# Row transform by pairs of column halves: a spectral layer and an MLP with all their gradients on one core

## The chip, the cores and the metric

The kernel runs on one NeuronCore of one Trainium2 chip. The core has five engines that run side by side, each with its own list of instructions: TensorE for matrix products (PE in the profile; its weight loads are listed as PEld), VectorE (DVE), ScalarE (ACT), GpSimd (POOL) and SyncE (SP). The last three also issue DMA transfers from their queues. The metric is the time of one execution on the device in microseconds; the kernel before takes 1196.34 us (median of 3 runs, 1196.11 to 1196.62).

## The reference

Two branches are computed from their inputs, mixed row by row by a sigmoid gate, and then everything is differentiated. S = 2048 rows, D = 1024 columns, F = 3584 hidden units; bf16 in and out.

```python
def _A_ref(x, w_r, w_i):
    X = rfft2(x.astype(float32), axes=(-2, -1))
    X = X * (w_r + 1j * w_i)                      # w: 2048 x 513
    return irfft2(X, s=(S, D), axes=(-2, -1)).astype(bfloat16)

def _B_ref(x, w1, b1, w2, b2):
    h = einsum("bsd,df->bsf", x, w1) + b1
    r = where(h > 0, h, 0)
    return einsum("bsf,fd->bsd", r * r, w2) + b2

x = A_x                                           # both branches read it; B_x is not used
g = sigmoid((x * gate_w).sum(-1, keepdims=True))
out = g * _A_ref(x, A_w_r, A_w_i) + (1 - g) * _B_ref(x, B_w1, B_b1, B_w2, B_b2)
_out, _vjp = jax.vjp(_f, A_x, A_w_r, A_w_i, B_w1, B_b1, B_w2, B_b2, gate_w)
return (_out, *_vjp(grad_out))
```

So nine arrays leave the kernel: the output and the gradients of x, of both filters, of the four MLP weights and biases, and of the gate.

## The kernel before

The two-dimensional Fourier transform is taken apart into small matrix products. Its stages run as a side task beside the MLP, which is the main task:

1. `first_stage` transforms x and the gated gradient along the columns and does the first part of the row transform; the result goes to a scratch array in HBM, `z_scr`.
2. `fft_mid` (line 333) does the rest of the row transform, multiplies by the filter, makes the gradient of the filter, and transforms back; its result goes to `y_scr`. **This is the stage that changes.**
3. `fft_out` reads `y_scr`, finishes the back transform and writes `ax_scr`, which the last stage (`Outputs`) adds to the MLP's result.

The MLP's main task is `mlp_in` (hidden layer and its gradient; products named ph, pZ and pd in the profile) until about 465 us, then `mlp_grads` (weight gradients; pX and pV), then `Outputs` (xX, xV, xZ). All three use a scheme of seven block products in place of eight, for which VectorE forms sums of operands (lines 873 and 1138) and joins of results. In `mlp_in` VectorE also makes each dhT (line 787, which frees the bank of a pd) and rT (line 900); ScalarE copies parts out of PSUM (cu, u: line 888) and squares (line 751).

The side task is a generator. `spread` advances it by a number of steps for every step of the main task: 1.5 side steps per main step while `fft_mid` runs beside `mlp_in` (`first_rate`), 1.2 times the main step's weight beside `mlp_grads` (`rate`). The tile framework then orders the recorded instructions for each engine and sets the semaphores. On each engine the instructions run in that order: one that waits holds up all behind it. A tile with a tag and `bufs=n` has n buffers that are used in turn; who writes a buffer again waits until its readers are done, DMA stores included.

`fft_mid` handles 16 pairs of row frequencies, m = 0 to 15, and each in two halves of the columns, h = 1 and then h = 0: 32 turns. A turn is:

- `inputs` (line 397): two DMAs on ScalarE's queue bring z for (m, h), two turns ahead.
- `mirrored` (line 419): on VectorE, sum and difference of the two parts of z into a tile pm (line 425; for m = 0, z itself).
- `transform` (line 430): four products px on TensorE, each of 128 partitions onto 64 (line 435), in a bank pair `ps2`; then ScalarE copies them out as x, once plain, once with the sign turned (lines 436 to 438).
- `by_groups` (line 407): GpSimd puts the filter's half in order (w), with its negative.
- `products` (line 441) and `joined` (line 449): VectorE multiplies x by w (two instructions, tt) and adds (y). The half h = 1 has one extra column, which is handed to h = 0 through eh.
- `back` (line 461): four products pv, each of 64 partitions onto 128 (line 466), in a bank pair `ps2`; ScalarE copies half of them (vc), VectorE makes sum and difference (pc, lines 472 and 473), GpSimd's queue stores them in `y_scr`.
- `grads_of_w` (line 478) and `grads_out` (line 489): VectorE multiplies and adds (g, gs), ScalarE scales into gw, and after h = 0 four stores on GpSimd's queue write the gradient of the filters.
- `filters` (line 388), once per m: five loads on GpSimd's queue, of the transform matrices (ab) and the filter rows (wn) for the next m.

The PSUM tag `ps2` has two buffers, and px and pv of all turns share them. `back` of a turn is issued in the next turn, so the order of TensorE's groups is px of turn u, then pv of turn u - 1, with products of the MLP between them nearly always.

Of the kernel before, what the change touches and what calls it, by code (L numbers as in the profile page):

```python
# [141 lines left out]
def kernel(  # L142
# [190 lines left out]
    def fft_mid(filler):  # L333
# [16 lines left out]
        def edges_through(ams):  # L350
            flat = lambda t_: t_[:].rearrange("p a b l -> p (a b l)")
            parted = fb.tile([P, 2, 2, HW], FDT, name="parted", tag="pm")
            parted = flat(parted)[:, 0 : 4 * P].rearrange("p (e k i) -> p e k i", e=4, i=NT)
            of_edge = edge[:].rearrange("p x t i -> p (x t) i").unsqueeze(2).to_broadcast([P, 4, 8, NT])
# [4 lines left out]
            for e in range(4):  # L359
                mm(pe[:, e, :], lhsT=parted[:, e].rearrange("p k i -> p (k i)"), rhs=row_of[:], start=True, stop=True, skip_group_check=True)  # L360
            ed = fb.tile([P, 2, 2, HW], FDT, name="ed", tag="y")
            ed = flat(ed)[:, 0 : NM * 8].rearrange("p (m n e) -> p m n e", n=2, e=4)
# [56 lines left out]
        def mirrored(m, z, summed=None):  # L419

            if m == 0:
                return z
            pm = fb.tile([P, 2, 2, HW], FDT, name="pm", tag="pm")
            for n, op in enumerate((ALU.add, ALU.subtract)):
                mixed = V(out=pm[:, n], in0=z[:, 0], in1=z[:, 1], op=op)
                behind(mixed, "DVE")
                after(mixed, summed, mybir.DependencyClass.NoSync)
            return pm

        def transform(m, h, pm, ex):  # L430
            x = fb.tile([P, 3, 2, WL], FDT, name="x", tag="x", bufs=2)
            px = fps.tile([P, 2, 2, HW], FP32, name="px", tag="ps2", bufs=2)
            for c in range(2):
                for n in range(2):
                    behind(mm(px[lanes[n], c], lhsT=mats[m][:, 0, n, lanes[c]], rhs=pm[:, n], start=True, stop=True), "PE")  # L435
            nc.scalar.copy(out=x[:, 1:3, :, 0:HW], in_=px[:])
            copied = nc.scalar.mul(out=x[:, 0, :, 0:HW], in_=px[:, 1], mul=-1.0)
            nc.scalar.copy(out=x[:, :, :, h * HW], in_=ex[:, m, :, :, h])
            return x, copied
# [9 lines left out]
        def joined(h, tt, eh):  # L449
            y = fb.tile([P, 2, 2, HW], FDT, name="y", tag="y")  # L450
            V(out=y[:], in0=tt[:, 0, :, :, 0:HW], in1=tt[:, 1, :, :, 0:HW], op=ALU.add)
# [8 lines left out]

        def back(m, h, y):
            pc = fb.tile([P, 2, 2, HW], FDT, name="pc", tag="pc", bufs=2)
            pv = fps.tile([P, 2, 2, HW], FP32, name="pv", tag="ps2", bufs=2)
            for c in range(2):
                for n in (1, 0):
                    mm(pv[:, n], lhsT=mats[m][lanes[n], 1, c, :], rhs=y[lanes[n], c], start=c == 0, stop=c == 1)
            if m == 0:
                done = nc.scalar.copy(out=pc[:], in_=pv[:])
            else:
                vc = fb.tile([P, 2, HW], FP32, name="vc", tag="vc")  # L470
                done = nc.scalar.copy(out=vc[:], in_=pv[:, 1])
                V(out=pc[:, 0], in0=pv[:, 0], in1=vc[:], op=ALU.add)  # L472
                V(out=pc[:, 1], in0=pv[:, 0], in1=vc[:], op=ALU.subtract)
# [28 lines left out]
        ams = [some_am(0), some_am(1)]  # L502
        turns = [(m, h) for m in range(NM) for h in (1, 0)]
        z = {0: inputs(*turns[0])}
        later["mid"] = True
# [4 lines left out]
        for _ in filler:  # L510
            yield
        pm, w = mirrored(0, z.pop(0)), by_groups(1, wn[0])
        held = eh = gw = summed = None
        z[1] = inputs(*turns[1])
        yield
        for u, (m, h) in enumerate(turns):
            if h:
                eh = fb.tile([P, 2, 2], FDT, name="eh", tag="eh")
            x, copied = transform(m, h, pm, ex)
            if u + 2 < len(turns):  # L520
                z[u + 2] = inputs(*turns[u + 2], copied)
            yield
            if u + 1 < len(turns):
                pm = mirrored(turns[u + 1][0], z.pop(u + 1), summed)
            if held:
                done = back(*turns[u - 1], held)
            tt = products(h, x, w)
            if u + 1 < len(turns):
                m2, h2 = turns[u + 1]
                w = by_groups(h2, wn[m2])  # L530
            yield
            held = joined(h, tt, eh)
            yield
            if u:
                grads_out(*turns[u - 1], gs, gw, done)
            gs, summed = grads_of_w(h, x)
            if h:
                gw = fb.tile([P, 2, LW], BF16, name="gw", tag="gw", bufs=2)
                if m + 1 < NM:
                    wn[m + 1] = filters(m + 1)  # L540
            yield
        done = back(*turns[-1], held)
        grads_out(*turns[-1], gs, gw, done)
        yield
# [1373 lines left out]
```

## Time and profile before

| | |
|---|---|
| time, median of 3 runs | 1196.34 us |
| the profiled execution's own time | 1203.86 us |
| its span, first to last instruction | 1202.1 us |
| granted clock of TensorE | 0.999 |
| PE busy | 1179.5 us |
| DVE busy | 893.5 us |
| ACT busy | 535.8 us |
| POOL busy | 375.9 us |
| px, first and last start | 232.3 and 582.6 us |
| pv, first and last start | 242.6 and 596.0 us |
| px products | 128, four to a turn |
| pv products | 128, four to a turn |

One execution is recorded by the profiler. Matrix products overlap: each is listed with its whole duration (379 ns for one with 512 columns), while the next starts 216 ns after it; so distances between starts tell more than the busy time. In the lists of groups, a name such as pd<-dbT,w2T says which tile is written from which; L783 is line 783. "Idle" is the time that an engine sat before an instruction, with what ended it.

### The profile page before, as it was taken

The page shows a single profiled execution, that of the slowest core. Times are in us where ns is not written, and L with a number is a line of the kernel's source. Part 1 is how long each engine was busy: PE and PEld are TensorE (multiplying, and loading weights), DVE is VectorE, ACT ScalarE, POOL GpSimd, SP SyncE. Part 2 cuts the span into 40 slices and gives each one's busy share as a digit, 9 for nine tenths or more (in the row PEclk, how much of TensorE's full clock was granted, in tenths as well). Part 3 has the DMA queues.
Part 4 walks back from the last instruction along what each step waited for, and adds up shares of the span by engine and source line. Part 5 has one row for each costly group of instructions (what it writes and reads, how often), then busy time and mean ns, then how long its engine had stood idle before and what let it go on. Part 6 is the DMA issues. An engine that isn't in the chain of part 4 may idle for free.

```text
span 1202.1 us, 19429 instructions
## 1 busy us (share of the span) xinstructions
PE 1179.5 (98%) x7181; PEld 636.1 (53%) x7275; DVE 893.5 (74%) x1598; ACT 535.8 (45%) x961; POOL 375.9 (31%) x618
## 2 busy tenths in 40 slices
PE   8989999999999999999999999999999999999998
PEld 5555555443333444444446899999544444444444
DVE  5878887689898887776637666666786677986757
ACT  5657888576767783444414556564201010000000
POOL 0224433665666663553322322321001100000000
PEclk9999999999999999999999999999999999999999
DMA  9998585686969888989897999994889999665530
GB/s 242 295 237 244 179 210 185 203 200 192 220 189 212 246 243 174 206 183 220 202 225 141 232 218 249 252 208 151 258 170 251 270 255 280 192 188 153 179 123 36
DMA packets 329464, 249.84 MB, mean 208 GB/s; under 512 B 187912, under 2 KB 287658, under 8 KB 328858
## 3 DMA queue, kind: packets, MB, share of 16 engines
q1 hardware_dynamic: 268352, 112.12, 44.8%
q0 software_dynamic: 35136, 111.72, 29.4%
q10 hardware_dynamic: 25882, 24.76, 7.3%
q8 instruction: 57, 0.93, 0.3%
q14 instruction: 37, 0.30, 0.1%
HBM read 114.82 MB, written 89.67 MB: 170 GB/s over the span
## 4 chain that ended last, share of the span: by engine, by line
PE 73%; DVE 12%; DMA 5%; ACT 4%; issue 4%; SPq 1%; POOL 0%; ACTq 0%; another core or an unknown queue 0%; DVEq 0%; POOLq 0%
PE pX L1206 15%; PE xX L1505 13%; PE pV L1206 11%; PE pd L783 8%; PE xV L1505 6%; PE ph L884 6%; PE xZ L1505 3%; DMA dhT_scr<-dhT 1%; PE pui L325 1%; DVE rT L900 1%; PE ph L776 1%; PE pki L591 1%; PE px L435 1%; DVE dhT L787 1%; DMA z<-z_scr 1%
## 5 line engine op out<-in xcount | busy, mean ns | idle before, releaser
L783 PE MATMUL pd<-dbT,w2T 128*128 128x512 bf16 x859 | 205.4, 379 | 4.4 <-DMA w2T<-in_B_w_dram 2.0
L783 PEld LDWEIGHTS <-w2T 128*128 128x128 bf16 x896 | 86.3, 98 | 106.4 <-issue 3.9
L1505 PEld LDWEIGHTS <-dS 128*128 128x128 f16 x686 | 66.3, 98 | 79.1 <-issue 3.4
L787 DVE SCALAR_TENSOR_TENSOR dhT<-pd,rT 128x512 bf16<-128x512 f32 x112 | 76.6, 684 | 32.7 <-PE pd L783 26.0
L1556 POOL DMA_DIRECT2D out_dram<-ot x32 | 17.3, 542 | 249.4 <-DVE ot L1612 128.0
L1622 ACT ACTIVATE w2br<-w2br,dsc 128x512 f32<-128x512 bf16 x8 | 5.8, 722 | 175.0 <-DVE ot L1612 117.4
L1222 ACT COPY u<-pX 128x512 f32<-128x512 f32 x56 | 32.8, 585 | 98.7 <-PE pX L1206 92.6
L1505 PE MATMUL xX<-oT,dS 128*128 128x512 f16 x336 | 76.5, 379 | 0.2 <-DVE eR L1534 0.2
L1505 PEld LDWEIGHTS <-odd 128*128 128x128 bf16 (+1 forms) x462 | 44.8, 98 | 51.5 <-issue 0.9
L1505 PEld LDWEIGHTS <-even 128*128 128x128 bf16 (+1 forms) x448 | 43.6, 98 | 52.6 <-issue 0.7
L1206 PEld LDWEIGHTS <-T 128*128 128x128 f16 x672 | 64.7, 98 | 7.9 <-issue 0.7
L901 ACT ACTIVATE rT<-rT 128x512 bf16<-128x512 bf16 x69 | 43.3, 628 | 40.7 <-DVE rT L900 40.7
L751 ACT ACTIVATE h2T<-rT 128x1024 bf16<-128x1024 bf16 x56 | 59.7, 1065 | 0.5 <-issue 0.2
L1226 DVE TENSOR_TENSOR whi<-pV,u 128x512 bf16<-128x512 f32 x28 | 19.3, 690 | 51.6 <-ACT u L1222 48.1
L475 POOL DMA_DIRECT2D y_scr<-pc x64 | 46.9, 734 | 34.4 <-DVE pc L472 31.9
L446 DVE TENSOR_TENSOR tt<-x,w 128x1028 f16<-128x1028 f16 (+1 forms) x64 | 41.9, 691 | 17.0 <-issue 12.5
L1206 PEld LDWEIGHTS <-S 128*128 128x128 f16 x336 | 32.3, 98 | 41.0 <-DVE S L1138 1.3
L1206 PEld LDWEIGHTS <-resL 128*128 128x128 bf16 x448 | 43.0, 98 | 4.7
L1206 PEld LDWEIGHTS <-resR 128*128 128x128 f16 (+1 forms) x448 | 42.9, 98 | 4.9 <-issue 0.2
L1206 PEld LDWEIGHTS <-even 128*128 128x128 bf16 (+1 forms) x256 | 24.5, 98 | 30.8 <-issue 2.1
L815 POOL DMA_DIRECT2D h2T_scr<-h2T x28 | 20.7, 738 | 62.1 <-ACT f L285 30.8
L499 POOL DMA_DIRECT2D out_dram<-gw x64 | 34.4, 543 | 17.8 <-ACT gw L495 13.9
(381 smaller groups left out, 2757.8 us busy)
## 6 DMA issues: line engine op xcount, KB each, us to landing
h2T_scr<-h2T POOLq DMA_DIRECT2D x28, 512.0 KB, 4.4
dhT_scr<-dhT POOLq DMA_DIRECT2D x28, 512.0 KB, 5.2
y_scr<-pc POOLq DMA_DIRECT2D x64, 128.0 KB, 3.9
ax_scr<-yo POOLq DMA_DIRECT2D x16, 512.0 KB, 5.4
out_dram<-ot POOLq DMA_DIRECT2D x31, 256.0 KB, 3.1
z<-z_scr ACTq DMA_DIRECT2D x60, 128.0 KB, 4.4
out_dram<-whi POOLq DMA_DIRECT2D x28, 256.0 KB, 5.3
out_dram<-wlo POOLq DMA_DIRECT2D x28, 256.0 KB, 5.2
```

The source lines that it names most:

```text
L446: V(out=tt[:, k, :, :, 0:W], in0=x[:, a : a + 2, :, 0:W], in1=by, op=ALU.mult)
L475: st(out=columns_of(y_scr, c, h), in_=pc[:, n])
L499: st(out=every(dst_w, k), in_=gw[lanes[n], c_, 0:W1])
L751: after(nc.scalar.activation(h2T, rT, ACT.Square), behind_, mybir.DependencyClass.NoSync)
L783: mm(pd[:], lhsT=w_[:, ec, fc % FGC * P : (fc % FGC + 1) * P], rhs=dbT[:, ec, ss], start=(ec == 0), stop=(ec == DC - 1),)
L787: return STT(out=dhT, in0=pd[:], scalar=2.0, in1=rT, op0=ALU.mult, op1=ALU.mult, accum_out=gb1part[:, fc, sb : sb + 1],)
L815: st(out=scr[2 * fp : 2 * fp + 2, :, cols2].rearrange("c p s -> p c s"), in_=t_[:])
L884: mm(acc[:], lhsT=lhs[:, t, :], rhs=rhs[:, t, :], start=start and t == 0, stop=t == KH - 1, skip_group_check=True)
L901: nc.scalar.activation(rT, rT, ACT.Relu)
L1206: self.mm = mm(out, lhsT=lhs[:, t, m * P : (m + 1) * P], rhs=rhs[:, t, :], start=start and t + a == 0, stop=t == KH - 1, skip_group_check= ...
L1222: turn["ACT"] = nc.scalar.copy(out=t_[:], in_=self.X[:])
L1505: ins = mm(acc, lhsT=lhs[:, fc, :], rhs=rhs[:, fc, :], start=start and fc == 0, stop=fc == KH - 1 and bias is None, skip_group_check=True,)
```

## The change

`fft_mid` works on both halves of one m together. The old `transform` is split: `spectra` issues the four px of a half, `transform` does the copies. The old `back` is split: `rows_of` issues the four pv, `back` the rest. For each m the order is now: px of both halves; copies and products of h = 1, then of h = 0; the filter gradient of h = 1; the sums of `mirrored` for both halves of the next m; pv of both halves; their copies, sums and stores; the filter gradient of h = 0; the gradient's scaling. The scaling and the stores for h = 0 are kept until the third step of the next m. There are still eight steps per m.

Buffers change with it. pm holds only the sum, with two buffers of half the size; the difference is written over z. y has two buffers in place of one, gw one in place of two. The loads of z for both halves of the next m are issued together, after the copies of h = 1; `filters` for the next m after those of h = 0.

```diff
-            parted = fb.tile([P, 2, 2, HW], FDT, name="parted", tag="pm")
+            parted = fb.tile([P, 2, HW], FDT, name="parted", tag="pm", bufs=2)
...
-            ed = fb.tile([P, 2, 2, HW], FDT, name="ed", tag="y")
+            ed = fb.tile([P, 2, 2, HW], FDT, name="ed", tag="y", bufs=2)
...
             if m == 0:
-                return z
-            pm = fb.tile([P, 2, 2, HW], FDT, name="pm", tag="pm")
-            for n, op in enumerate((ALU.add, ALU.subtract)):
-                mixed = V(out=pm[:, n], in0=z[:, 0], in1=z[:, 1], op=op)
+                return z[:, 0], z[:, 1]
+            pm = fb.tile([P, 2, HW], FDT, name="pm", tag="pm", bufs=2)
+            for out, op in ((pm[:], ALU.add), (z[:, 1], ALU.subtract)):
+                mixed = V(out=out, in0=z[:, 0], in1=z[:, 1], op=op)
                 behind(mixed, "DVE")
                 after(mixed, summed, mybir.DependencyClass.NoSync)
-            return pm
-
-        def transform(m, h, pm, ex):
-            x = fb.tile([P, 3, 2, WL], FDT, name="x", tag="x", bufs=2)
+            return pm[:], z[:, 1]
+
+        def spectra(m, pm):
             px = fps.tile([P, 2, 2, HW], FP32, name="px", tag="ps2", bufs=2)
             for c in range(2):
                 for n in range(2):
-                    behind(mm(px[lanes[n], c], lhsT=mats[m][:, 0, n, lanes[c]], rhs=pm[:, n], start=True, stop=True), "PE")
+                    behind(mm(px[lanes[n], c], lhsT=mats[m][:, 0, n, lanes[c]], rhs=pm[n], start=True, stop=True), "PE")
+            return px
+
+        def transform(m, h, px, ex):
+            x = fb.tile([P, 3, 2, WL], FDT, name="x", tag="x", bufs=2)
             nc.scalar.copy(out=x[:, 1:3, :, 0:HW], in_=px[:])
...
-            y = fb.tile([P, 2, 2, HW], FDT, name="y", tag="y")
+            y = fb.tile([P, 2, 2, HW], FDT, name="y", tag="y", bufs=2)
...
-        def back(m, h, y):
-            pc = fb.tile([P, 2, 2, HW], FDT, name="pc", tag="pc", bufs=2)
+        def rows_of(m, y):
             pv = fps.tile([P, 2, 2, HW], FP32, name="pv", tag="ps2", bufs=2)
             for c in range(2):
                 for n in (1, 0):
                     mm(pv[:, n], lhsT=mats[m][lanes[n], 1, c, :], rhs=y[lanes[n], c], start=c == 0, stop=c == 1)
+            return pv
+
+        def back(m, h, pv):
+            pc = fb.tile([P, 2, 2, HW], FDT, name="pc", tag="pc", bufs=2)
...
-        for u, (m, h) in enumerate(turns):
...
+        for m in range(NM):
+            more = m + 1 < NM
+            eh = fb.tile([P, 2, 2], FDT, name="eh", tag="eh")
+            px = {h: spectra(m, pm[h]) for h in (1, 0)}
+            w[0] = by_groups(0, wn[m])
+            x, y, gs, pv, summed = {}, {}, {}, {}, {}
+            x[1], copied = transform(m, 1, px[1], ex)
+            if more:
+                z = {h: inputs(m + 1, h, copied) for h in (1, 0)}
+            yield
+            tt = products(1, x[1], w[1])
+            y[1] = joined(1, tt, eh)
+            x[0], _ = transform(m, 0, px[0], ex)
+            if more:
+                wn[m + 1] = filters(m + 1)
+            yield
+            tt = products(0, x[0], w[0])
+            if last_:
+                grads_out(*last_)
+            yield
+            y[0] = joined(0, tt, eh)
+            yield
+            gs[1], summed[1] = grads_of_w(1, x[1])
+            yield
+            if more:
+                pm = {h: mirrored(m + 1, z[h], summed[1]) for h in (1, 0)}
+            pv = {h: rows_of(m, y[h]) for h in (1, 0)}
+            back(m, 1, pv[1])
+            yield
+            done = back(m, 0, pv[0])
+            gs[0], summed[0] = grads_of_w(0, x[0])
+            if more:
+                w[1] = by_groups(1, wn[m + 1])
+            yield
+            gw = fb.tile([P, 2, LW], BF16, name="gw", tag="gw")
+            grads_out(m, 1, gs[1], gw, done)
+            last_ = (m, 0, gs[0], gw, done)
+            yield
+        grads_out(*last_)
```

More of the change, by code (lines that the diff above doesn't have):

```diff
@@ L351, in edges_through @@
             flat = lambda t_: t_[:].rearrange("p a b l -> p (a b l)")
-            parted = fb.tile([P, 2, 2, HW], FDT, name="parted", tag="pm")
-            parted = flat(parted)[:, 0 : 4 * P].rearrange("p (e k i) -> p e k i", e=4, i=NT)
+            parted = fb.tile([P, 2, HW], FDT, name="parted", tag="pm", bufs=2)
+            parted = parted[:].rearrange("p b l -> p (b l)")[:, 0 : 4 * P].rearrange("p (e k i) -> p e k i", e=4, i=NT)
             of_edge = edge[:].rearrange("p x t i -> p (x t) i").unsqueeze(2).to_broadcast([P, 4, 8, NT])
@@ L502, in fft_mid @@
         ams = [some_am(0), some_am(1)]
-        turns = [(m, h) for m in range(NM) for h in (1, 0)]
-        z = {0: inputs(*turns[0])}
+        z = {1: inputs(0, 1)}
         later["mid"] = True
@@ L511, in fft_mid @@
             yield
-        pm, w = mirrored(0, z.pop(0)), by_groups(1, wn[0])
-        held = eh = gw = summed = None
-        z[1] = inputs(*turns[1])
+        w = {1: by_groups(1, wn[0])}
+        z[0] = inputs(0, 0)
+        pm = {h: mirrored(0, z[h]) for h in (1, 0)}
+        last_ = gw = None
         yield
-        for u, (m, h) in enumerate(turns):
[L517 to L521, printed above, removed]
-            yield
[L523 to L530, printed above, removed]
+        for m in range(NM):
[7 more added lines that the diff above has]
+                z = {h: inputs(m + 1, h, copied) for h in (1, 0)}
+            yield
+            tt = products(1, x[1], w[1])
[3 more added lines that the diff above has]
+                wn[m + 1] = filters(m + 1)
@@ L531, in fft_mid @@
             yield
-            held = joined(h, tt, eh)
+            tt = products(0, x[0], w[0])
+            if last_:
+                grads_out(*last_)
             yield
[L534 to L540, printed above, removed]
-            yield
-        done = back(*turns[-1], held)
@@ L543, in fft_mid @@
-        grads_out(*turns[-1], gs, gw, done)
+            y[0] = joined(0, tt, eh)
+            yield
+            gs[1], summed[1] = grads_of_w(1, x[1])
[9 more added lines that the diff above has]
+                w[1] = by_groups(1, wn[m + 1])
```

## The prediction

> **What bounds the kernel now.** I read the page first (engines, chain of waits), then busy time by stretch, then the timelines of PE and DVE inside the stage that changes.
>
> ```profile
> PE 1179.5 (98%) x7181; PEld 636.1 (53%) x7275; DVE 893.5 (74%) x1598; ACT 535.8 (45%) x961; POOL 375.9 (31%) x618
> PE 73%; DVE 12%; DMA 5%; ACT 4%; issue 4%; SPq 1%; POOL 0%; ACTq 0%; another core or an unknown queue 0%; DVEq 0%; POOLq 0%
> ```
>
> PE is busy 98% of the span and carries 73% of the chain that ended last. A change in one stage is worth what it does to PE's own time there, as long as PE does not begin to wait. The stage runs from the first px (232.3 us) to the last pv (596.0); the stretches around it:
>
> ```profile
> 250.00:300.00 50.00, 49.15 (x235) 19.90 (x238) 44.21 (x93) 36.34 (x64) 31.36 (x50) 1.00 0.81 204
> 300.00:350.00 50.00, 48.57 (x232) 19.64 (x235) 45.21 (x96) 37.22 (x66) 32.18 (x50) 1.00 0.87 215
> 350.00:400.00 50.00, 49.64 (x237) 19.97 (x241) 44.94 (x100) 36.16 (x62) 35.65 (x57) 1.00 0.84 194
> 400.00:450.00 50.00, 49.64 (x238) 20.27 (x242) 41.89 (x92) 38.99 (x70) 32.47 (x51) 1.00 0.85 254
> 450.00:500.00 50.00, 49.37 (x234) 20.98 (x237) 41.75 (x66) 19.78 (x35) 24.03 (x38) 1.00 0.92 194
> 500.00:550.00 50.00, 49.73 (x238) 20.70 (x240) 35.08 (x56) 22.37 (x40) 22.04 (x36) 1.00 0.80 174
> ```
>
> Columns: stretch, its length, then busy us of PE, PEld, DVE, ACT, POOL, the granted clock (full), DMA share, GB/s. Up to about 460 the row transform runs beside the MLP's first half, and DVE is about as full (45 of 50) as PE; after that it has 9 to 15 of 50 us free. PE's idle time in these six rows adds to 3.9 us: that is all that better waits could give. The cost of the transform's products stands in PE's timeline:
>
> ```profile
> 300.47 1.89 PE L783 MATMUL pd<-dbT,w2T 128*128 128x512 bf16 x8
> 302.29 0.62 PE L435 MATMUL px<-pm,ab 128*64 128x512 f16 x4
> 302.85 0.61 PE L466 MATMUL pv<-y,ab 64*128 64x512 f16 x4
> 303.38 1.90 PE L783 MATMUL pd<-dbT,w2T 128*128 128x512 bf16 x8
> ...
> 416.85 1.03 PE L884 MATMUL ph<-dbn,Sw 128*128 128x512 f16 x4
> 417.81 0.61 PE L466 MATMUL pv<-y,ab 64*128 64x512 f16 x4
> 418.35 1.04 PE L884 MATMUL ph<-dbn,Sw 128*128 128x512 f16 x4
> ```
>
> Full products start every 0.216 us (8 in 1.73). The last pd starts at 300.47 + 7 x 0.216 = 301.98; the first px follows 0.31 later, not 0.216. The px run two at a time, as two pairs 0.24 apart; then another 0.31 to the first pv, its pairs 0.225 apart, and 0.31 to the next pd. So each change of the array's shape (128*128, 128*64, 64*128) costs PE about 0.1 us in which nothing starts, though the page counts it as busy. The weight loads show the same pause:
>
> ```profile
> 302.29 0.14 PEld L435 LDWEIGHTS <-ab 128*64 128x64 f16 x4 [0.42 <-issue]
> 302.84 0.12 PEld L466 LDWEIGHTS <-ab 64*128 64x128 f16 x4 [0.41 <-issue]
> 303.38 1.41 PEld L783 LDWEIGHTS <-w2T 128*128 128x128 bf16 x8 [0.42 <-issue]
> ```
>
> Between one weight load and the first of another shape PEld sits 0.41 to 0.42 us; between loads of one shape it is 0.12.
>
> **The change, part by part.**
>
> *Products put together (PE).* A lone group of four px costs 0.31 + 0.24 + 0.31 - 0.216 = 0.65 us, a lone group of four pv 0.85 - 0.216 = 0.63, and px with pv behind it 303.38 - 301.98 - 0.216 = 1.18, 0.10 less than apart. In the order of the instructions, before has 31 px groups of four and one split 1 + 3, 32 pv groups, nine pv directly behind px: 121 changes of shape. The changed kernel has 15 px groups of eight and 2 of four, 11 pv groups of eight and 10 of four (a few full products stand between the halves): 76 changes. Before: 31 x 0.65, the split group 0.4 + 0.65 (a lone px is 0.31 + 0.31 - 0.216), 32 x 0.63, less 9 x 0.10: 40.5 us. A group of eight, estimated from the same steps: px 0.31 + 3 x 0.24 + 0.31 - 0.216 = 1.12, pv 0.31 + 3 x 0.225 + 0.31 - 0.216 = 1.08. After: 15 x 1.12 + 2 x 0.65 + 11 x 1.08 + 10 x 0.63 = 36.3 us. **Gain 4.2 us.** No row shows eight in a row, so its middle is bounded: from the 0.24 between pairs up to the 0.31 of a change of shape, 26 x 0.08 = 2.1 us less gain. I take 0.24, since the step stays within one shape.
>
> [...] In the row above, the second pair's weights load at 302.29 to 302.43, while the first pair (from 302.29) still streams. [...]
>
> *Sums in place, pm half as wide, two buffers.* The same four L425 sums per m, 0.42 each: nothing in DVE's work. "DVE pm waits for PE px" (5.1 us, 5 times) goes, because a second pm exists. All four now stand together.
>
> *y with two buffers, filters earlier.* "DVE y waits for PE pv" (2.0 us) goes; so does "POOL ab waits for PE pv" (11.6 us), as filters(m+1) is issued after the pv of m-1. None of these engines ends the chain here: 0, from -0.5 to 0.
>
> *Both px, then both pv, share the two ps2 banks, and vc has one buffer.* The second px waits for the last pc of the m before; the second vc waits for the first half's two pc. Behind the waiting ACT copy stand the MLP's copies u and cu, which PE's next products need. From DVE's timeline, successive sums start 0.60 apart (pc at 306.80, 307.40, dhT at 308.00), L425 0.34 apart, the reduction 1.13. Chain from a pv pair to the freed bank: vc 0.6 + pc 1.2 + vc 0.6 + pc 1.2 = 3.6 us, plus what DVE does between. The order leaves 24 to 40 full products, 5.2 to 8.6 us, before the next px: covered, if DVE is at most 2 us late.
>
> *DVE's order around the pv.* This is the tight place. Once in three m, between the last half's y and the dhT of the next pd, DVE now has dhT, an operand sum, g, pc, gs, four pm, pc, dhT: 0.6 + 0.34 + 0.6 + 0.6 + 0.34 + 1.34 + 0.6 + 0.68 = 5.1 us. Before, the longest such run I find goes from the dhT at 296.36 to the end of the one at 300.63, 4.95 us, without any L425 in it. PE meanwhile has a pv group, 0.53, and 22 products, 4.75: 5.3 us. Then two operand sums, the reduction and rT, 0.67 + 1.13 + 0.7 = 2.5 us, against 8 products, 1.73: PE waits about 0.5 us. Four such places: 2 us. Elsewhere I find cover. Before has 3.9 us of such stalls in other places; some go. I set the two against each other: 0, from -3.9 (all go, none come) to +11 (1 us in each of 11 m).
>
> *z loads.* Four at once on ACT's queue, 0.37 us each to issue, beside the copies already running; landing 4.4 us (up to 11.7) against some 13 us to the sums. 0.
>
> *gw with one buffer.* ACT's next write to gw waits for four stores of the last m. Usually they are over 10 us old. Once in three m they are issued about 6 us before: 0.54 each on POOL's queue, landing 5.3 after (up to 9.3). ACT waits about 1.5 us there, and DVE's pc a little; PE has some 2 us of slack: 0, up to 2 us each when they land late.
>
> **Sum.** Profiled execution 1203.86 us (span 1202.1, 1.8 around it): -4.2 gives 1199.7. That execution is 7.5 us above the median, and no view says where those lie; I take the gain as it is: 1196.34 - 4.2 = **1192.1 us**.
>
> **Rivals.**
> 1. *DVE sets the pace up to 460, or the inner steps cost as a change of shape.* For: DVE 45 of 50. Against: 5 us are free. Only the last five m, with free DVE, keep their gain: 5 x (2.56 - 2.20) = 1.8 us: 1194.5. Inner steps at 0.31: 1194.2.
> 2. *DVE's longer run makes PE wait* (slower). Place: pd products behind the dhT that follows four pm. For: 5.1 us of sums against 5.3 of cover, and 2.5 against 1.73 right behind. Against: DVE can use its idle time to begin early. At 1 us in 11 m: +11 - 4.2 = +6.8: 1203.1. It decides from 0.6 us per m.
> 3. *gw's stores land late.* For: one store took 9.3 us. Four times 2 us: +8 - 4.2 = +3.8: 1200.1.
>
> **Numbers.** Forecast 0.45, rival 1 0.25, rival 2 0.2, rival 3 0.1. Within 0.2% (2.4 us, about what a measurement of this kernel can tell from none) lies rival 1 with a little of it outside: faster 0.48, same 0.22, slower 0.30. The forecast's own range is 1188 (all stalls gone) to 1194. With rivals 2 and 3 half in: 1187.5 to 1203.
>
> **What would show it.** px and pv groups of eight taking 1.1 us from full product to full product, inner steps of 0.24; PE idle in 250 to 460 no more than before; POOL's wait for pv gone. Wrong would be: PE idle behind dhT or rT, ACT waiting for stores of gw with u or cu late, or inner steps above 0.3.

## The result, and the profile after

The changed kernel takes 1203.0 us (median; single executions lie between 1199.5 and 1211.8), the kernel before 1196.4 (1195.3 to 1204.2) on the same chip: a ratio of 1.0054, with a 95% interval of 1.0037 to 1.0072. It is slower by 6.6 us. The forecast was 1192.1, with a range that ended at 1203.0 and 0.3 for slower. Of all the executions below, the figures leave out one slow one, 1212.2 us at a granted clock of 0.993 (the best kernel with one tile of gw), 1.5% above that kernel's fastest.

The profiled execution of after took 1206.56 us (span 1204.7). Its page first, engines and chain:

```profile
PE 1181.0 (98%) x7275; PEld 639.0 (53%) x7275; DVE 893.2 (74%) x1598; ACT 532.8 (44%) x961; POOL 383.1 (32%) x618
PE 55%; DVE 7%; issue 3%; DMA 3%; ACT 1%; POOL 1%; ACTq 0%; DVEq 0%; POOLq 0%
```

The busy times are those of before within 2%. The two chains cannot be compared by their shares: this one is traced back only to 358.8 us, its shares add to 70% of the span, and PE's 55% is about four fifths of that (before: 73% of a chain that covers nearly all of the span). The stretches show where PE waits (columns as in the prediction):

```profile
250.00:300.00 50.00, 47.36 (x231) 19.62 (x229) 43.70 (x93) 34.80 (x65) 33.88 (x52) 1.00 0.79 206
300.00:350.00 50.00, 48.84 (x240) 20.52 (x238) 46.41 (x101) 34.92 (x63) 34.47 (x54) 1.00 0.93 207
350.00:400.00 50.00, 45.76 (x221) 19.00 (x220) 39.47 (x89) 34.89 (x63) 32.34 (x50) 1.00 0.83 190
400.00:450.00 50.00, 47.95 (x228) 19.66 (x226) 40.10 (x89) 33.81 (x59) 30.70 (x47) 0.97 0.76 223
450.00:500.00 50.00, 47.84 (x229) 20.20 (x228) 40.51 (x64) 21.32 (x36) 23.75 (x36) 1.00 0.88 202
500.00:550.00 50.00, 50.00 (x245) 21.72 (x244) 35.55 (x57) 22.68 (x44) 27.01 (x40) 1.00 0.93 183
```

Between 250 and 500 us PE is idle 12.3 us (before: 3.6), in the last row not at all. One more thing has to be taken out before spans are compared. The code ahead of the stage is the same in both kernels, yet one and the same dhT of it, the 40th, starts at 201.8 us in the profile of before and at 195.5 in that of after (in the 18 traces of the other runs at 193.3 to 199.2). So most of the 7.5 us by which the profiled execution of before lay above its median, some 6.3, passed ahead of the stage. From that dhT to the start of the MLP's last one (466.6 and 471.4) after is 11.1 us longer, from there to the end 2.2 shorter. The change gains where the row transform runs beside the next stage, and loses five times as much beside the MLP. (This execution of after lies 3.6 us above its median, so its stalls add to more than the 6.6 us.)

**The products.** PE's timeline around a px group of eight (the two matmuls of a pair start together, one of each is shown):

```profile
306.95 1.02 PE L901 MATMUL ph<-dbn 128*128 128x512 f16 x4 [0.29 <-DVE rT L917]
307.90 0.40 PE L434 MATMUL px<-pm,ab 128*64 128x512 f16 x1
...
308.14 0.38 PE L434 MATMUL px<-pm,ab 128*64 128x512 f16 x1
...
308.36 0.38 PE L434 MATMUL px<-pm,ab 128*64 128x512 f16 x1
...
308.57 0.38 PE L434 MATMUL px<-pm,ab 128*64 128x512 f16 x1
...
308.89 1.04 PE L901 MATMUL ph<-dbn 128*128 128x512 f16 x4
```

The last ph starts at 307.60; then come steps of 0.31, 0.24, 0.21, 0.21 and 0.31: the group costs 1.28 - 0.216, 1.07 to 1.08 us. A pv group of eight costs 1.05 to 1.07 in the same way (steps of 0.31, 0.22, 0.21, 0.21 and 0.31). By the upper figures the products take 15 x 1.08 + 2 x 0.65 + 11 x 1.07 + 10 x 0.63 = 35.6 us instead of 40.5: they gain 4.9 us.

**The stalls.** What took it back stands in the waits of 230 to 470 us (total us, times, longest):

```profile
ACT gw L501 <- DMA out_dram<-gw: 8.4, 4, 3.2
ACT vc L477 <- DVE pc L479: 7.2, 7, 1.5
...
DVE tt L449 <- ACT x L439: 6.1, 5, 1.8
...
ACT eh L458 <- DVE en L457: 5.6, 5, 2.2
...
DVE dbn L890 <- DMA w1g<-in_B_w_dram: 1.9, 1, 1.9
```

The first, the second and the last are not among the waits of before. Three kinds of stall follow from them, counted by how much longer a step from one product to the next is than 0.216 us. Between 230 and 480 us the steps over 0.45 us add to 15.3 us by this count, in before to 4.3.

First, gw's one tile. The chain of waits, then PE:

```profile
380.65 7.25 DMA out_dram<-gw
...
388.01 0.21 ACT gw L501
388.22 0.47 ACT vc L477
388.69 0.49 ACT u L905
```

```profile
389.23 1.02 PE L901 MATMUL ph<-dbn,Sw 128*128 128x512 f16 x4 [1.01 <-ACT u L905]
```

A store of the last gw is on its way for 7.25 us, ACT stands 2.75 us for it, the copies vc and u come behind it, PE waits for u. With the px that then wait for pc (0.56 at 392.9) this place costs 1.7 us. No stall of PE stands right behind the other three of the four waits, of 1.1, 1.4 and 3.2 us.

Second, the sums right behind the px. DVE's timeline around 352 us and what PE waits for:

```profile
349.71 0.73 DVE L917 SCALAR_TENSOR_TENSOR rT<-ph,b1col,u 128x512 bf16<-128x512 f32 x1
...
352.12 1.31 DVE L449 TENSOR_TENSOR tt<-x,w 128x1028 f16<-128x1028 f16 x2 [1.59 <-ACT x L439]
353.46 0.69 DVE L454 TENSOR_TENSOR y<-tt 128x1024 f16<-128x1024 f16 x1
354.06 0.60 DVE L457 TENSOR_TENSOR en<-tt 128x4 f16<-128x4 f16 x1
354.59 0.68 DVE L804 SCALAR_TENSOR_TENSOR dhT<-pd,rT 128x512 bf16<-128x512 f32 x1
```

```profile
355.33 0.38 PE L800 MATMUL pd<-dbT,w2T 128*128 128x512 bf16 x1 [1.67 <-DVE dhT L804]
```

DVE stands 1.59 us for half 1's x, with the MLP's dhT queued behind tt, tt, y and en. (The px had ended at 350.1 us; x started at 351.0, because ACT first waited 0.49 us for DVE's rT and worked on that.) Stalls of this kind, where PE waits for dhT or rT behind these sums, or for one of the MLP's copies behind ACT's eh and half 0's x, add to 8.6 us (1.25 at 273.7, 0.87 and 0.80 at 293 to 296, 0.58 at 336, 1.83 at 355, 0.93 at 399, 0.87 and 1.47 at 464 to 467).

Third, one late load: w1g landed 11.0 us after its issue (before: 4.0 to 4.1 where its landing shows), a sum of it came late, then y, and pv waited 2.1 us at 426.1. What came behind that stall was new to me; the rows are in the last section.

### The profile page after: what moved, and what is told of

Same layout as the page of the kernel before. It is cut to its first block, busy times and chain, and to the rows that moved or that the text cites. A ratio compares the mean times of both kernels' runs of the same rounds, so it can differ in the third digit from the quotient of the medians.

```text
span 1204.7 us, 19497 instructions
## 1 busy us (share of the span) xinstructions
PE 1181.0 (98%) x7275; PEld 639.0 (53%) x7275; DVE 893.2 (74%) x1598; ACT 532.8 (44%) x961; POOL 383.1 (32%) x618
## 4 chain that ended last, share of the span: by engine, by line
PE 55%; DVE 7%; issue 3%; DMA 3%; ACT 1%; POOL 1%; ACTq 0%; DVEq 0%; POOLq 0%
PE pX L1223 15%; PE xX L1522 13%; PE pV L1223 11%; PE xV L1522 7%; PE xZ L1522 3%; PE pui L325 1%; PE pki L608 1%; PE ph L901 1%; PE pd L800 1%; DMA w1g<-in_B_w_dram 1%; DVE S L1155 1%; DMA dhT_scr<-dhT 1%; DMA out_dram<-gw 1%; DVE oT L1470 1%; DVE ot L1562 0%
## 5 line engine op out<-in xcount | busy, mean ns | idle before, releaser
L800 PE MATMUL pd<-dbT,w2T 128*128 128x512 bf16 x896 | 212.0, 380 | 5.9 <-DVE dhT L804 4.6
L1522 PEld LDWEIGHTS <-even 128*128 128x128 bf16 (+1 forms) x448 | 43.7, 98 | 52.6 <-issue 0.7
L449 DVE TENSOR_TENSOR tt<-x,w 128x1028 f16<-128x1028 f16 (+1 forms) x64 | 41.9, 693 | 22.4 <-issue 13.3
L410 POOL COPY w<-wn 128x512 bf16<-128x512 bf16 x32 | 30.0, 937 | 41.9 <-DVE tt L449 39.8
L901 PEld LDWEIGHTS <-w1g 128*128 128x128 bf16 x252 | 24.1, 98 | 32.3 <-issue 6.3
```

Of the source, the lines that this page charges most:

```text
L410: G.tensor_copy(out=w[:, 0:2, 0:HW].rearrange("p c (g i) -> p c g i", g=4), in_=wn[:, :, h * HW : (h + 1) * HW].rearrange("p c (i g) -> p ...
L449: V(out=tt[:, k, :, :, 0:W], in0=x[:, a : a + 2, :, 0:W], in1=by, op=ALU.mult)
L800: mm(pd[:], lhsT=w_[:, ec, fc % FGC * P : (fc % FGC + 1) * P], rhs=dbT[:, ec, ss], start=(ec == 0), stop=(ec == DC - 1),)
L901: mm(acc[:], lhsT=lhs[:, t, :], rhs=rhs[:, t, :], start=start and t == 0, stop=t == KH - 1, skip_group_check=True)
L1522: ins = mm(acc, lhsT=lhs[:, fc, :], rhs=rhs[:, fc, :], start=start and fc == 0, stop=fc == KH - 1 and bias is None, skip_group_check=True,)
```

## The experiments

All times are medians beside the kernel before on the same chip, 1196.3 to 1196.7 us. Ratios are to that kernel; they are not ratios of the medians, and where executions spread widely a difference of two medians and that of their ratios can differ by some us.

### What gw's one tile costs

**Another place for gw.** No memory is added: gw shares three equal tiles with wn.

```diff
-            wn = fb.tile([P, 2, LW], BF16, name="wn", tag="wn", bufs=2)
+            wn = fb.tile([P, 2, LW], BF16, name="wn", tag="wn", bufs=3)
-            gw = fb.tile([P, 2, LW], BF16, name="gw", tag="gw")
+            gw = fb.tile([P, 2, LW], BF16, name="gw", tag="wn", bufs=3)
```

> The changed kernel with one edit: gw takes its memory in turn with wn from three equal tiles, so that a new gw no longer waits for the stores of the last one; the order of PE, DVE, ACT and SP is unchanged. Theory A, that the time was lost where ACT waits for the stores of gw: the changed kernel's trace shows that wait 4 times, 8.4 us in all, and PE stalls right behind one of them (at 389.2 us, 1.17 us above the usual step, and 0.56 at 392.9). The wait disappears from ACT and the time falls by about 1.7 us, to 1201.3; by the prediction's rival 3 as it stood (four times 2 us) it would fall by 8, to 1195. Theory B, that the loss lies behind the px, where ACT stands at eh until DVE has made en, with the MLP's copies behind it: the wait disappears, the time stays within 2 us of 1203.0.

Measured: 1205.8 us, 1.0075 [1.0056, 1.0094]. ACT's wait for the stores was gone and the stall at 389 too, but POOL now waited 26.0 us for loads of wn, w1g landed 15.5 us after its issue and PE stalled 7.4 us for it. The wait had only moved to another queue; nothing follows for gw's price.

**Two tiles of gw.** The room comes from vc, which goes (in FP16) into a part of half 1's x that is no longer read.

```diff
-                vc = fb.tile([P, 2, HW], FP32, name="vc", tag="vc")
+                vc = spare[:, 0, :, 0:HW]        # spare is x[1]
-            gw = fb.tile([P, 2, LW], BF16, name="gw", tag="gw")
+            gw = fb.tile([P, 2, LW], BF16, name="gw", tag="gw", bufs=2)
```

> The changed kernel with gw in two tiles of its own, as before the change. The room for it: vc (in FP16 now) lies in the part of x of half 1 that is read no more, and stays one buffer. The order on PE, DVE, ACT and SP is that of the changed kernel but for a few places. Theory A (ACT waits for the stores of gw, 8.4 us in the changed kernel, up to 12.4 in the kernels tried since, and PE stalls of 1.4 to 5.3 us stand right behind the longest of these waits): the wait goes, the time falls by 2 to 5 us, to 1198 to 1201. In the run with gw and wn in turn the wait had gone too, but there the loads of wn waited for the stores (POOL waited 26.0 us for wn) and the load of w1g landed 15.5 us after its issue; if theory A is right, it was this that made up for the gain. Theory B (hand-over behind the px): stays, so the time does not get to that of before, 1196.4.

Measured: 1200.7 us, 1.0034 [1.0011, 1.0057]; once more, beside another run:

> The kernel with gw in two tiles once more, beside the run above: 1200.7 as before, its executions between 1196 and 1208.

1198.0 us, 1.0032 [1.0013, 1.0051]. The wait is gone; against 1203.0 that is 2.3 and 5.0 us by medians, 2.4 and 2.6 by the ratios, and the intervals of both ratios overlap that of the changed kernel, so these two runs alone do not prove a gain. Single executions spread over 12 us in both kernels. The place of vc and the order of DVE and ACT change a little with this edit, too. In its profile (the execution of 1196.85 us) PE's long steps add to 9.1 us instead of 15.3; those behind the px are among what shrank, from 8.6 to 5.8.

**One tile in the kernel before.**

```diff
-                gw = fb.tile([P, 2, LW], BF16, name="gw", tag="gw", bufs=2)
+                gw = fb.tile([P, 2, LW], BF16, name="gw", tag="gw")
```

> The kernel before with one part of the change alone: gw in one tile instead of two. The orders of PE, DVE, POOL and SP stay the same, ACT's but for a few places. Theory A (one gw costs by itself): ACT waits for the stores, PE stalls behind it, 1198 to 1202. If the cost needs the new order (the four stores issued late in m, behind other stores of POOL's queue): the same as before within 1 us, 1196.4.

Measured: 1221.3 us, 1.0204 [1.0172, 1.0236]: 24.7 us slower, with PE, DVE, POOL and SP in the same order. Its waits and one place in ACT's timeline:

```profile
ACT gw L495 <- DMA out_dram<-gw: 10.2, 2, 5.4
ACT gw L490 <- DMA out_dram<-gw: 9.7, 3, 4.7
```

```profile
302.23 0.58 ACT L471 COPY vc<-pv 128x512 f32<-128x512 f32 x1 [0.20 <-PE pd L783]
307.51 1.09 ACT L490 ACTIVATE gw<-gs 128x512 bf16<-128x512 f16 x1 [4.69 <-DMA out_dram<-gw]
```

Behind each of these five waits (1.8 to 5.4 us; five more, of up to 11.9, come behind 480 us) PE stalled 1.8 to 5.0 us. I expected at most 6 us in all. One tile is dear in either order.

**One tile in the best kernel** (the one at the end of this section), every engine's order the same:

> The run with the steps spread, eh on DVE and dhT first (1193.5), with gw in one tile as in the changed kernel; every engine's order stays the same. Theory A (one tile of gw costs by itself, because ACT stands until the four stores have landed, with the MLP's copies behind): ACT waits for the stores again, 8 to 15 us in all, single PE stalls of 2 to 5 us, 1198 to 1206. If the price of one tile was that of the changed kernel's order (2.3 us there): 1195 to 1197.

Measured: 1201.9 us (1194.0 to 1211.6), 1.0044 [1.0018, 1.0069], against 1193.5 (1192.5 to 1198.2), 0.9975 [0.9961, 0.9989]: 8.4 us (8.3 by the ratios), and the executions spread three times as wide. The profiled execution, one of the shorter ones, has a single such stall (a second wait, of 2.0 us at 443.5, stalls nothing); ACT, then PE:

```profile
322.90 0.21 ACT L502 ACTIVATE gw<-gs 128x2 bf16<-128x2 f16 x1 [3.98 <-DMA out_dram<-gw]
...
324.93 0.59 ACT L906 COPY u<-ph 128x512 f32<-128x512 f32 x1
```

```profile
325.57 1.02 PE L902 MATMUL ph<-xT,dbn 128*128 128x512 f16 x4 [3.16 <-ACT u L906]
```

The same copies with two tiles, where ACT waits only for DVE's sum:

```profile
319.64 0.21 ACT L502 ACTIVATE gw<-gs 128x2 bf16<-128x2 f16 x1 [0.98 <-DVE gs L493]
...
321.71 0.58 ACT L906 COPY u<-ph 128x512 f32<-128x512 f32 x1
```

This pair is the cleanest answer: nothing differs but the tile, and the orders of all engines in the two traces are the same.

### One half of the change alone

**Forward pairs only**, first with one tile of gw, then with two. In the second kernel half 1's vc overwrites part of x before that half's gradient of the filter is formed, so out_3, one of the filters' two gradients, is not the reference's; the work and its order are as described.

```diff
+            back(m, 1, rows_of(m, y[1]))          # behind products(0, ...)
...
-            pv = {h: rows_of(m, y[h]) for h in (1, 0)}
-            back(m, 1, pv[1])
-            yield
-            done = back(m, 0, pv[0])
+            yield
+            done = back(m, 0, rows_of(m, y[0]))
```

> The changed kernel with the forward products of both halves together as now, and each half's back products and sums pc by themselves again (half 1's behind half 0's element-wise products). 104 changes of the array's shape instead of 76, 121 before: 1.7 us of the product gain is left. Theory B (hand-over behind the px): the loss stays, 1196.3 - 1.7 + 8.6 = 1203. Theory C (DVE's run of sums around the two pv): the loss goes, 1194.6 to 1197.

> One half of the change on even ground: two tiles of gw, the forward products of both halves together, each half's back products by themselves. With gw in one tile it took 1212.6, with stores of gw keeping ACT for 8.8 us and a PE stall of 4.3 us behind them. 104 changes of shape instead of 121: 1.7 us gain by the products. If gw's one tile was its whole loss: 1195 to 1197. If the forward pairs cost by the hand-over behind the px as well: 1198 to 1204.

Measured: 1212.6 us, 1.0134 [1.0117, 1.0151], and 1204.5 us, 1.0059 [1.0036, 1.0083]. The second tile (with vc's new place) takes 8.0 us off, and a loss of 7.8 stays: what is left of the change here, the forward pairs with their loads and their order, costs by itself. DVE's run of sums around the pair of pv (the prediction's rival 2) cannot be the whole of the loss, since this kernel has no such pair.

**Back pairs only**, two tiles of gw: each half's px by itself, half 0's behind y of half 1.

```diff
-            px = {h: spectra(m, pm[h]) for h in (1, 0)}
...
-            x[0], _ = transform(m, 0, px[0], ex)
+            x[0], _ = transform(m, 0, spectra(m, pm[0]), ex)
```

> The other half on the same ground: two tiles of gw, the back products of both halves together, the forward products of half 0 given after half 1's sum y (in 4 of 16 m they still come directly behind half 1's). 102 changes of shape, 1.9 us gain by the products. If the back pairs cost by DVE's run of sums around them (the prediction's rival 2): 1200 to 1204. If the loss lies behind the px pairs: 1194 to 1197.

Measured: 1199.4 us, 1.0020 [1.0006, 1.0035]: 2.7 us slower than before, between the two expectations. The back pairs are the cheaper half, but no gain either. The halves do not add up: with two tiles of gw the losses are 7.8 and 2.7 us alone, and 4.2 and 1.6 in the two runs with both. So each order makes waits of its own, and these runs do not divide the 6.6 us between the pairs.

### What stands behind the px

**eh on DVE**, with one tile of gw and with two.

```diff
-                nc.scalar.mul(out=eh[:, 0], in_=en[:, 1], mul=-1.0)
-                nc.scalar.copy(out=eh[:, 1], in_=en[:, 0])
+                nc.vector.tensor_scalar(out=eh[:, 0], in0=en[:, 1], scalar1=-1.0, scalar2=None, op0=ALU.mult)
+                nc.vector.tensor_copy(out=eh[:, 1], in_=en[:, 0])
```

> The changed kernel with one edit: the two small copies that make eh out of en go from ACT to DVE, right behind en. ACT then waits for no sum of DVE between the two halves' x. Theory B (the loss lies in the hand-over behind the px: x of half 1, its products and sum, en, eh, x of half 0, each waiting for the other engine): the changed trace has ACT waiting for en 5 times, 5.6 us; the stalls of PE right behind it add to 8.6 us (1.25 at 273.7, 0.87 and 0.80 at 293 to 296, 0.58 at 336, 1.83 at 355, 0.93 at 399, 0.87 and 1.47 at 464 to 467). Those behind ACT (2.6 us at 273.7, 296.5 and 336) should go, the others shrink: 1195 to 1200. Theory A (stores of gw) and theory C (DVE's run of sums around the pv): no change, 1203, or a little more for 32 more small instructions of DVE.

> Both edits: gw in two tiles of its own, eh made on DVE. If the two causes add (stores of gw 2 to 5 us, ACT standing at eh some 4 us: the stalls at 273.7, 336 and 464 to 467 us were gone or short in the run with eh on DVE alone, where the wait for the stores of gw grew from 8.4 to 12.4 us), the time comes to 1195 to 1198. If eh does nothing, the same as with gw alone.

Measured: 1204.7 us, 1.0072 [1.0060, 1.0085], and 1202.5 us, 1.0051 [1.0029, 1.0072]. ACT waits for en no more, and in the first the stalls at 274 and 336 are gone, but those of 1.9 us behind dhT (294.8, 356.4) stay, and the wait for gw's stores grew to 12.4 us, with a stall of 5.0 us behind it. In the second PE waits for rT instead (1.4 us at 340.7, 1.6 at 402.0). ACT's wait for en alone was not the cause.

**x of half 0 ahead of half 1's products.**

```diff
             x[1], copied = transform(m, 1, px[1], ex)
+            x[0], _ = transform(m, 0, px[0], ex)
...
             y[1] = joined(1, tt, eh)
-            x[0], _ = transform(m, 0, px[0], ex)
```

> The changed kernel with one edit: x of half 0 is made right behind x of half 1, ahead of half 1's products, so that on ACT the copies of x of half 0 stand before eh. Two waits of the hand-over behind the px are taken apart: ACT makes both x without DVE, DVE finds the second x ready. All products of the middle are paired but one group. Theory B (hand-over behind the px): most of its 8.6 us go, 1194 to 1199. Theory C (DVE's run of sums around the pv, the prediction's rival 2): 1203, since that run stays as it is. Against both: 3.2 us of x copies in a row on ACT may make the MLP's copies late in a new place.

Measured: 1214.8 us, 1.0148 [1.0132, 1.0163]: a miss in the other direction. gw's stores keep ACT 10.7 us here (longest 6.4, with a stall of 5.1 us behind), and DVE waits 9.5 us for loads of z. With one tile of gw this says little on x.

**The steps spread:** y of half 1 one step of the MLP behind its products, the steps behind it one later; also two tiles of gw, eh on DVE and two places for vc.

```diff
             tt = products(1, x[1], w[1])
+            yield
             y[1] = joined(1, tt, eh)
...
-            yield
             gw = fb.tile([P, 2, LW], BF16, name="gw", tag="gw", bufs=2)
```

> As the run before it, with vc in two places of x too, and half 1's sum y one step of the MLP later than its products (before, the two stood in different steps; the changed kernel has products, sum and edges of half 1 in one), the steps behind it one later. If the stalls of 2.1 us behind dhT (at 293 to 296 and 355 in the changed kernel, once in three m) come from the run of DVE's tt, tt, y, en with the MLP's dhT behind it, they go, and the time is 1191 to 1194, below that of before. If they come from elsewhere (late transfers), 1196 to 1198 as without it.

Measured: 1198.1 us, 1.0011 [0.9996, 1.0027]. Against 1202.5 without these edits it wins 4.4 us, and the intervals do not meet. How much of that is vc's second place, which took away a wait of ACT's of 7.6 us in all, was not tried. PE still waited 2.0 us for y at 290.4, 2.0 for dhT at 354.4 and 1.5 for cu at 415.0.

**dhT ahead of tt.** One order more: half 1's tt behind the MLP's last dhT that is written down before them.

```diff
-                V(out=tt[:, k, :, :, 0:W], in0=x[:, a : a + 2, :, 0:W], in1=by, op=ALU.mult)
+                made = V(out=tt[:, k, :, :, 0:W], in0=x[:, a : a + 2, :, 0:W], in1=by, op=ALU.mult)
+                after(made, later["last"] if h else None, mybir.DependencyClass.NoSync)
```

> The changed kernel with gw in two tiles (as in the run with gw alone, 1200.7) and one order more: DVE's products tt of half 1 stand behind the MLP's last dhT that is written down ahead of them. Theory E (once in three m DVE stands idle 1.6 us for x of half 1, with tt, tt and y ahead of a dhT whose pd is done; PE waits 2.05 us at 352.2 and 1.1 + 1.0 at 291 to 294 in that run): these three stalls go or are under 0.6, the time falls by 2 to 3.5 us, to 1197 to 1199. If tt then is late and pv waits for y instead: the stalls move behind y, 1200 to 1202.

> The run with two tiles of gw, eh on DVE and the steps spread (1198.1), with the same order more: tt of half 1 behind the last dhT. Its stalls of 2.17 at 290.4 (pv waits for y), 2.25 at 354.4 (pd waits for dhT) and 1.72 at 415.0 (ph waits for cu) are what keeps it from the time that the products alone would give: theory E takes away the one at 354.4 and perhaps that at 415.0, and the time comes to 1194 to 1196.5, at or below before. If late transfers set the rest, 1197 to 1199.

Measured: 1199.6 us, 1.0021 [1.0007, 1.0035], which is not to be told from two tiles alone; and 1193.5 us, 0.9975 [0.9961, 0.9989], which beats the kernel before by 0.25% and is the best of all. In the first the stalls behind dhT are gone, but pv waits for y in their place (2.0 us at 421). In the second the stall at 354 is gone and little came for it; those at 290 and 415 shrank to 0.3 and 0.7 us. DVE and PE around the same products:

```profile
348.42 0.69 DVE L805 SCALAR_TENSOR_TENSOR dhT<-pd,rT 128x512 bf16<-128x512 f32 x1 [1.14 <-PE pd L801]
349.04 0.08 DVE L805 DVE_READ_ACCUMULATOR dhT<-pd,rT 128x1 f32 x1
349.04 0.69 DVE L449 TENSOR_TENSOR tt<-x,w 128x1028 f16<-128x1028 f16 x1
```

```profile
350.29 1.02 PE L902 MATMUL ph<-dbn,Sw 128*128 128x512 f16 x4 [0.53 <-ACT cu L906]
```

DVE uses the time in which x is being made for dhT, and PE waits 0.7 us there instead of 2.0. Its first four stretches, beside those of after above:

```profile
250.00:300.00 50.00, 48.92 (x236) 20.82 (x240) 46.52 (x103) 33.88 (x59) 36.30 (x58) 1.00 0.80 203
300.00:350.00 50.00, 48.59 (x233) 20.46 (x236) 45.74 (x100) 35.85 (x60) 33.17 (x51) 1.00 0.92 206
350.00:400.00 50.00, 48.40 (x230) 20.75 (x234) 44.69 (x105) 36.22 (x61) 35.04 (x53) 1.00 0.82 205
400.00:450.00 50.00, 48.99 (x241) 20.73 (x245) 41.35 (x92) 37.02 (x61) 34.00 (x53) 1.00 0.77 245
```

PE is idle 5.1 us in these 200 us; in after it was 10.1.

**The same two order edits on the kernel before.**

> The kernel before with the two order edits that need no pairs: eh on DVE, and DVE's products of half 1 behind the last dhT. If the gain of the best run (3.2 us) comes from the paired products (they save 4.9 us by the rows of the trace) once the waits are gone: here the same as before, 1195 to 1198. If it comes from the order edits: 1192 to 1195.

Measured: 1197.7 us, 1.0007 [0.9996, 1.0018]. The edits give nothing there (the steps stand spread in that kernel anyway). So the 3.2 us of the best kernel most likely belong to the pairs, once the waits that they bring are out of the way; its new buffers were not tried alone.

**One step later still**, with half 0's x ahead of half 1's products.

> As the best run, with half 1's products tt one step of the MLP later still and its x of half 0 ahead of them. If what is left of the stalls (eight of 0.6 to 1.0 us) comes from DVE's sums standing too close behind the px: 1191 to 1193. If the back products get late in turn (8 of the groups of eight come apart again: 78 changes of shape instead of 72, 0.6 us): 1194 to 1197.

Measured: 1202.0 us, 1.0037 [1.0024, 1.0050]: too late. pv waits for y at 260, 321 and 383 us (1.1, 0.5 and 1.1), and at the end of the MLP PE stood 4.2 us for an operand sum, which is the larger part.

### Loads

**Half 0's z one step later**, in the best kernel.

```diff
-                z = {h: inputs(m + 1, h, copied) for h in (1, 0)}
+                z = {1: inputs(m + 1, 1, copied)}
...
-            x[0], _ = transform(m, 0, px[0], ex)
+            x[0], copied = transform(m, 0, px[0], ex)
+                z[0] = inputs(m + 1, 0, copied)     # if more
```

> The run with the steps spread, eh on DVE and dhT first (1193.5), with half 0's two loads of z issued one step later, behind the copies of its own x, instead of four loads in a row. Theory F (the bunched loads make the transfers beside them late, w1g's above all: 4.0 us before, 4.7 to 15.5 in the runs with all four in a row): w1g lands in 4 to 6 us, and the time falls by up to 2 us, 1191.5 to 1193. If the loads are no cause: 1193.5 within 1 us.

Measured: 1210.2 us, 1.0086 [1.0055, 1.0118]: the opposite of what I expected. Its waits:

```profile
DVE pm L425 <- DMA z<-z_scr: 19.3, 5, 7.5
PE px L434 <- DVE pc L480: 14.3, 5, 6.4
```

The four sums pm stand on DVE's queue ahead of pc, so late loads stop pc, and with it the px that wait for the bank (6.6 and 6.2 us at 334 and 404). The four loads in a row are what the four sums in a row need.

They have a price that I overlooked. ACT issues them itself, and its copies come behind. From the best kernel, ACT and then PE:

```profile
407.76 2.26 ACTq L404 DMA_DIRECT2D z<-z_scr  x2
410.06 0.58 ACT L906 COPY cu<-ph 128x512 f32<-128x512 f32 x1 [1.75 <-PE pd L801]
```

```profile
410.70 1.02 PE L902 MATMUL ph<-dbn,Sw 128*128 128x512 f16 x4 [0.51 <-ACT cu L906]
```

The copy starts 0.04 us behind the end of the last issue. Two more of the stalls that the best kernel has left, at 289.3 and 350.3 us, also wait for a cu that starts 0.04 us behind such an issue: 0.7 us each. In the changed kernel six copies start like that, after 0.5 to 1.9 us in which ACT was idle; no stall of PE that I list stands right behind them. What the issues cost in all, no run here shows.

**w1g ahead of the fourth load of dbn.** SyncE's queue in the changed kernel:

```profile
402.52 9.35 SPq L1089 DMA_DIRECT2D dbn<-db_scr  x4
411.96 0.39 SPq L823 DMA_DIRECT2D w1g<-in_B_w_dram  x1
```

```diff
-                again(slice(2 * low, 2 * low + 2), later["last"])
+                again(slice(2 * low, 2 * low + 2), later["last"], later["w1"] if low == 3 else None)   # NoSync behind that load of w1
```

> The changed kernel with gw in two tiles, and the last load of w1g ahead of the fourth load of dbn on SyncE's queue, where it stood before the change. Theory G (the late w1g is a cause of its own): it lands in 4 to 8 us instead of 9.8 to 11, the stall of pv for y at 420 to 426 us goes (1.0 to 2.3 us, and some 1.5 us more where products of 427 ns instead of 216 follow it), the time falls by 1 to 4 us against the same kernel without the swap. Otherwise both are the same within 1 us.

Measured: 1199.3 us, 1.0030 [1.0013, 1.0047], beside 1198.0 without the swap. In the profile the stall for y (1.2 us at 421 in the run beside it) is gone, and from dhT to dhT the MLP is 1.2 us shorter; the medians and the ratios do not show it. As a cause of the 6.6 us it stays unproven.

## Why the prediction was wrong, step by step

- **Products put together: right, 0.7 us too small.** 4.9 us instead of 4.2: the inner steps are 0.24, 0.21 and 0.21, two of them below both of my bounds. The gain is there behind 470 us (2.2 us), and most likely in the 3.2 us of the kernel without the waits.
- **Sums in place, pm and y with two tiles: right.** DVE's waits of 5.1 and 2.0 us for px and pv are gone, and POOL's for pv is 6.5 instead of 11.6. None ended anything.
- **Two banks and one vc: nearly right.** I called it covered. px waited for pc at two places (0.53 and 0.56 us), ACT 7.2 us for vc's tile, mostly off the path.
- **DVE's order: the step that failed by its place.** I had worked out DVE's run between the last y and the next dhT, and set its 2 us against stalls that would go. That run is there as I listed it (from the dhT at 299.3 to the rT at 306.2), and PE waits 0.45 us behind it, where I had said 0.5; but it does so once, not four times (in such a run at 366.3 another product waits 0.41 for pc). The run that hurt was the one behind the px, which I put at nothing: x of half 1 late on ACT, then tt, tt, y and en ahead of a dhT that was ready, 8.6 us of stalls in eight places. Before the change a step of the MLP stood between products and sum; the change put both into one step, and I never listed it. Spreading the steps (with vc's second place) and then putting dhT first showed it: 4.4 and 4.6 us, with the gw tiles held at two. That rival 2's 1203.1 is nearly the measured 1203.0 is luck: it had the stalls behind the four pm.
- **z loads: 0, right for the sums that need them.** DVE does not wait for z in the changed kernel; in the best kernel, half of the loads one step later cost 16.7 us by medians, 13.3 by the ratios. But I took 0.37 us for an issue; in the changed kernel it is 0.48 (median, up to 1.86), and copies of ACT stand behind it.
- **gw with one tile: the step that failed by size.** I wrote "ACT waits about 1.5 us there" and "PE has some 2 us of slack: 0, up to 2 us each when they land late". ACT waited 2.1 us on average and up to 3.2 (up to 6.5 in the other paired kernels with one tile), with stores that landed up to 9.8 us after issue. The slack was about 1.6 us in one place, where 2.75 us of waiting stalled PE for 1.2, and over 3 in another; of the five waits of 3.8 to 6.5 us in the other paired kernels four stalled PE, by 3.3 to 5.1. In runs the tile is worth 2.3 to 5.0 us in the changed order (2.4 and 2.6 by the ratios, not clear of noise), 8.0 with forward pairs only, 8.4 in the best order, where nothing else differs, and 24.7 in the order before. It was the third rival, which I gave 0.1 and 3.8 us net.
- **The sum.** The forecast's base was fair; the 7.5 us that I could not place lay ahead of the stage for the most part. With -4.9 for the products and +2.3 to +5.0 for gw's tile, the rest must come to 6.5 to 9.2 us to give the +6.6. The profile has 8.6 us behind the px and, at the late load of w1g, 2.1 us and 1.5 more behind it; how the rest divides between these two is not settled, because each edit of order moved both, and the stalls behind the px shrank with gw's second tile as well.

## What to carry to other kernels

When a change takes a second buffer away from something that a store reads, price it by the longest landing in the trace, not the median, and ask what stands behind the waiting copy on its engine (in after, vc and u behind the gw that waited 2.75 us): here a tile of 2 KB per partition was worth 2 to 8 us in the paired orders, where the products together gained 5. When work is put together for one engine, list the runs that come together on every other engine, each with what is queued behind it, not only the run beside the edit. And put the short eviction that the main engine waits for ahead of the long sums that still wait for their own input.

## What the hardware did that I had not expected

A stall of 2.1 us cost PE another 1.5 us behind its end. The stretches around the step of 2.28 us between two products in after (the stall at 426.1) (the column behind POOL's is the granted clock):

```profile
424.00:426.00 2.00, 0.20 (x1) 0.00 (x0) 1.97 (x5) 0.29 (x2) 1.26 (x2) 1.00 0.69 247
426.00:428.00 2.00, 1.90 (x9) 0.67 (x10) 2.00 (x6) 0.84 (x2) 2.00 (x4) 0.84 0.06 18
428.00:430.00 2.00, 2.00 (x6) 0.76 (x5) 2.00 (x7) 0.21 (x1) 2.00 (x4) 0.50 0.56 158
430.00:432.00 2.00, 2.00 (x8) 0.79 (x7) 2.00 (x6) 1.56 (x3) 1.43 (x3) 0.80 0.45 105
```

The granted clock falls to 0.50, and seven products follow each other at 427 ns instead of 216: 1.5 us more, which the page counts as busy time. The other long steps of after between 230 and 480 us, eight of 1.01 to 2.05 us, were followed by the usual 216 ns. In other traces 0.50 stands behind stretches in which PE did nothing:

| | PE did nothing (us) | granted clock 0.50 (us) |
|---|---|---|
| one tile in the kernel before | 259 to 261 | 263 to 265 |
| the same | 306 to 308 | 308 to 312 |
| forward pairs only, one tile of gw | 391 to 393 | 393 to 397 |
| gw in wn's tiles | 420 to 424 | 422 to 430 |
| half 0's z one step later | 329 to 333 | 335 to 339 |

But in the best kernel with one tile of gw four products behind a step of 3.54 us (the ph at 325.57 above) took 0.86 us, the usual 216 ns each. Why the clock fell in the one case and not in the other, no run here shows. In whole executions a lower clock goes with a longer time: in the first run with two tiles of gw the five executions with a granted clock of 1.000 took 1196.2 to 1198.3 us, the five with 0.995 to 0.997 took 1204.6 to 1208.2.
